# Turning the second half's attention probabilities: one set of products over 40 rows for both layers, placed behind the whole dense sum

## The chip, the cores and the metric

One NeuronCore of a Trainium2 chip runs the whole program. The metric is the device time of one execution in microseconds (us). A core has a matrix engine (TensorE, "PE" in the profile, with its weight loads listed apart as "PEld"), a vector engine (DVE), a scalar engine (ACT), a general engine (POOL), and a queue engine (SP) that issues most transfers. Each engine works through its own instructions in order; they meet at semaphores. SBUF is the on-chip memory of 128 rows (partitions); PSUM is the small memory into which PE writes its products and from which DVE and ACT copy them out.

## The reference

Two layers of memory-augmented attention, each followed by a dense block. The sequence of 2048 tokens is cut into 64 segments of 32; in front of each segment stand 8 memory tokens, which the attention itself rewrites from segment to segment, so the segments of a layer are a chain.

```python
def _A_ref(x, mem0, Wq, Wk, Wv, Wo, seg_len):      # H=32 heads, Dh=128, M=8, seg=32
    L = M + seg_len                                # 40
    mask = (idx[:, None] < M) | (idx[:, None] >= idx[None, :])
    for s in range(n_seg):
        h = concatenate([mem, xs])                 # 40 tokens
        q, k, v = h @ Wq, h @ Wk, h @ Wv           # per head
        p = softmax(where(mask, q k^T * scale, -1e9))
        o = (p v) @ Wo
        mem = o[:, :M]
        outs.append(o[:, M:])

def _B_ref(x, w1, w2):
    return relu(x @ w1) @ w2                       # 512 -> 1376 -> 512

x = x + _A_ref(_layernorm(x), ...)
x = x + _B_ref(_layernorm(x), ...)
x = x + _A_ref(_layernorm(x), ...)
x = x + _B_ref(_layernorm(x), ...)
```

## The kernel before

The two attention layers run interleaved: in step k, layer a=0 handles segment k and layer a=1 handles segment k-4. Steps 1 to 3 and 64 to 67 have one layer only, steps 4 to 63 have both; step 0 is written out apart. One step is some 23 us.

In a step the 32 heads are worked in two halves of 16. For each half, queries and keys of both layers come from one product (`qk`, line 591, 80 columns: 2 x 40 tokens), `scores` makes 40x40 scores per head and layer (line 625), and `exponentials` and `softmax` turn them into probabilities. A score tile has, per layer, two heads side by side on the partitions (rows 0 to 39 and 64 to 103, called g) and eight slots (s) in the free dimension: 128 x 8 x 40 = 128x320. The maximum, the subtraction and the row sum are on DVE (lines 643, 647, 659), the exponential on ACT (649), and the final multiplication by the reciprocal of the sum (664) on POOL, except for layer 1 of the second half, which is on DVE.

The product of probabilities and values needs the probabilities with the keys on the partitions, so they are turned. The first half's are turned by a transfer (`turn_p`, line 682). The second half's are turned on PE by `transpose_p(1, ...)`: for each of the 8 slots and each layer, a 128x64 slice of the tile `P1_sb` is loaded as weights and multiplied by an identity of 80 columns (line 675). The products of the two layers go to the two column halves of the array, so layer 0's keys land on PSUM rows 0 to 39 and layer 1's on rows 64 to 103. Two copies bring the result to `PT_sb` (line 679): ACT takes the first five slots (128x400), DVE the last three (128x240); in one-layer steps it is four and four.

Then `weighted_v` (line 701) runs 64 products, alternating between the layers (rows 0 to 39 and 64 to 103), 40 columns each. The first 16 heads read `PT0`, which the transfer filled; the last 16 read `PT_sb`, one head of each g per slot. `outputs` (719) copies the results to `OTm` (memory tokens) and `OTx` (the other tokens), `output_mem` (633, tile `wo`) multiplies `OTm` by Wo, and `new_memory` makes the next step's memory from it.

PE's work in the shadow of the softmax is the output product of the step before (`block`, 373), the dense block of an earlier segment (`dense_h`, 522; `dense_y`, 543). `dense_y` sums 11 chunks of the hidden dimension, two products of 256 columns for each chunk, in the two column halves of the array. In two-layer steps nine chunks stand ahead of the transposition and the last two behind it. `add_output(k-1)` on DVE adds the output product to the residual; it stands in DVE's order ahead of the PT copies.

The orders of PE, DVE, SP and POOL are those of the program text (`manual_schedule`, with `high_priority` blocks); ACT's is made by the scheduler. PSUM tiles come from pools: `ps_c` with three banks serves `tp`, `qp`, `vm` and some of the `pv` tiles.

`XN` is a 128x512 tile for the normalized rows. `normalize_step` fills it on DVE at the end of a step (in one-layer steps, and in step 4, early in the step itself); `transpose_step`, early in the step, turns it by a transfer into `xnT`, from which everything else reads.

The core of step k behind the second half's scores:

```python
        f_mid = 9 if ahead or k == 2 else 5
        if k < LAST:
            dense_y(k - 2, 0, f_mid)
        if not single:
            add_output(k - 1)
        ...
        with tc.high_priority(offset=PRIO):
            transpose_p(1, 4 if single else 5)
        if ahead and k < LAST:
            dense_y(k - 2, f_mid, NFC)
        tokens_in(k + 1)
        ...
            pvs = weighted_v(act)
            outputs(k, pvs)
```

Of the kernel before, what the change touches and what calls it, by code (L numbers as in the profile page):

```python
# [7 lines left out]
BF = mybir.dt.bfloat16  # L8
F32 = mybir.dt.float32
ALU = mybir.AluOpType  # L10
# [12 lines left out]
def kernel(  # L23
# [14 lines left out]
    nc = tc.nc  # L38
    _, S, Dm = A_x.shape
    _, H, Dh = A_Wq.shape[0], A_Wq.shape[1], A_Wq.shape[2]  # L40
# [4 lines left out]
    L = M + SEG  # L45
    NSEG = S // SEG
    assert NSEG % 4 == 0 and DELTA == 4
    LAST = NSEG + DELTA - 1
    NXT = NSEG // 4
    NC4 = Dm // 128  # L50
    NFC = (Dff + 127) // 128
# [5 lines left out]
    const = ctx.enter_context(tc.tile_pool(name="const", bufs=1))  # L57
    wk = ctx.enter_context(tc.tile_pool(name="wk", bufs=2))
    dram = ctx.enter_context(tc.tile_pool(name="vdram", bufs=2, space=DRAM))
    ps_c = ctx.enter_context(tc.tile_pool(name="ps_c", bufs=3, space=PSUM))  # L60
# [11 lines left out]
    def has1(k):  # L72
        return DELTA <= k <= LAST
# [22 lines left out]
    def span(d):  # L96
        offs = ([0] if has0(d) else []) + [o for o, _ in slots_of.get(d, [])]
        return base(d) + min(offs), base(d) + max(offs) + 32
# [65 lines left out]
    ident = const.tile([128, 128], BF)  # L164
# [3 lines left out]
    ident_q = ident[:].rearrange("p (g q) -> p g q", g=2)[:, :, 0:L]  # L168
# [22 lines left out]
    XN = const.tile([128, Dm], BF)  # L191
# [3 lines left out]
    Vs = const.tile([128, H * Dh], BF)  # L195
    P_sb = const.tile([128, 8, 128], BF)
    nc.gpsimd.memset(P_sb[:], 0.0)
    P1_sb = const.tile([128, 16 * L + 24], BF)
    nc.gpsimd.memset(P1_sb[:], 0.0)
    PT_sb = const.tile([128, 8, 2, L], BF)  # L200
    PT0 = const.tile([128, 8, 128], BF)
    OTx = const.tile([128, H, 64], BF)
# [6 lines left out]
    for a in range(2):  # L209
        t = ps_s.tile([128, 512], F32, name=f"sp{a}")  # L210
# [24 lines left out]
    def moments_x(n):  # L235
        return stat_tail(stats_x(n), "x")
# [295 lines left out]
    def dense_y(d, f0, f1, bank=1):  # L532
        if not 0 <= d <= LAST:
            return
        lo, hi = span(d)
        n = hi - lo
        for fc in range(NFC)[f0:f1]:
            fs = 128 if fc < NFC - 1 else F_LAST
            for j in range(2):


                w = 8 * L if fc == 0 else 256
                nc.tensor.matmul(sp_banks[bank][64 * j:64 * j + n, 0:w], lhsT=hT_tiles[d][0:fs, fc, 0:n],  # L543
                                 rhs=w2_flat[0:fs, fc * Dm + 256 * j:fc * Dm + 256 * j + w],
                                 start=(fc == 0), stop=(fc == NFC - 1), skip_group_check=True,
                                 tile_position=(0, 64 * j))
# [68 lines left out]
    def masks(*act):  # L615
        for a in act:
            nc.vector.tensor_copy(out=sp_tiles[a], in_=maskb2)  # L617
# [20 lines left out]
    def exponentials(act):  # L638
        mxs, ess = {}, {}
        for a in act:  # L640
            sp = sp_tiles[a]
            mxs[a] = wk.tile([128, 8], F32, tag="mx", bufs=2, name="mx")
            nc.vector.tensor_reduce(out=mxs[a][:], in_=sp, axis=AX.X, op=ALU.max)  # L643
        for a in act:
            sp = sp_tiles[a]
            es = ess[a] = wk.tile([128, 8, L], F32, tag="es", bufs=2, name="es")
            nc.vector.tensor_tensor(out=es[:], in0=sp, in1=mxs[a][:].unsqueeze(2).to_broadcast([128, 8, L]),  # L647
                                    op=ALU.subtract)
            last_exp[0] = nc.scalar.activation(out=es[:], in_=es[:], func=ACTF.Exp, scale=SCALE)  # L649
        return ess  # L650

    def softmax(hf, act, by_pe=False, ess=None):
        if ess is None:
            ess = exponentials(act)
        if by_pe and hf:
            transpose_p(0)
        for a, es in ess.items():
            sm = wk.tile([128, 8], F32, tag="sm", bufs=2)
            nc.vector.tensor_reduce(out=sm[:], in_=es[:], axis=AX.X, op=ALU.add)  # L659
            nc.vector.reciprocal(out=sm[:], in_=sm[:])  # L660
            eng = nc.vector if by_pe or (hf, a) == (1, act[-1]) else nc.gpsimd
            P = P1_sb[:, 0:16 * L].rearrange("p (s a q) -> p s a q", s=8, a=2)[:, :, a, :] if hf else \
                P_sb[:, :, 64 * a:64 * a + L]
            eng.tensor_tensor(out=P, in0=es[:],  # L664
                              in1=sm[:].unsqueeze(2).to_broadcast([128, 8, L]), op=ALU.mult)

    def transpose_p(hf, cut=4):

        for s0, ns, copy in ((0, cut, nc.scalar.copy), (cut, 8 - cut, nc.vector.tensor_copy)):
            tp = ps_c.tile([128, ns, 2, L], F32, tag="c", name="tp")  # L670
            for sl in range(ns):
                for a in range(2):
                    c = L * (2 * (s0 + sl) + a)
                    P = P1_sb[:, c:c + 64] if hf else P_sb[:, s0 + sl, 64 * a:64 * a + 64]
                    nc.tensor.matmul(tp[64 * a:64 * a + 64, sl], lhsT=P, rhs=ident_q,  # L675
                                     start=True, stop=True, tile_position=(0, 64 * a))
            PT = PT_sb[:, s0:s0 + ns] if hf else \
                PT0[:, s0:s0 + ns].rearrange("p s (g q) -> p s g q", g=2)[:, :, :, 0:L]
            copy(out=PT, in_=tp[:])

    def turn_p():
        nc.sync.dma_start_transpose(out=PT0[:], in_=P_sb[:].rearrange("p s k -> p (s k)"))
# [3 lines left out]
    def weighted_v(act):  # L686
        pvs = {}
        for t, (h0, nh) in enumerate(PVS):
# [6 lines left out]
            for hi in range(nh):  # L695
                hf, hh = divmod(h0 + hi, 16)
                sl, g2 = divmod(hh, 2)
                for a in act:
                    R = 64 * a
                    PT = PT_sb[R:R + L, sl, g2, :] if hf else PT0[R:R + L, sl, 64 * g2:64 * g2 + L]  # L700
                    nc.tensor.matmul(pvs[t, a][:, hi, :], lhsT=Vs[R:R + L, (h0 + hi) * Dh:(h0 + hi + 1) * Dh],  # L701
                                     rhs=PT, start=(hi == 0 or (t, a) != (1, 1)), stop=True,
                                     skip_group_check=(t, a) == (1, 1))
# [181 lines left out]
    def first_step():  # L885


        slots = iter([w1_flat[:, 512 * i:512 * i + 512] for i in range(NC4 * Dff // 512)] +
                     [w2_flat[:, 512 * i:512 * i + 512] for i in range(8)])
        masks(0)  # L890
        with tc.high_priority(offset=PRIO):
            qks = qk(0, [0])
            scores(qks, [0])
            softmax(0, [0], True)
            values_first(0)
            memory_values(0, (next(slots), None), (0,))
            values_second(0, next(slots))
            values0(1, 0, stage=next(slots))
            values0(1, 2, stage=next(slots))
            m = moments_x(2)  # L900
            normalize(nc.vector, xbs[2], xbs[2], m, 0, 128)
            inputs_T(2)
            values0(3, 0, stage=next(slots))
            values0(3, 2, stage=next(slots))
            load_x(1)
            qks = qk(1, [0], between=lambda: values0(5, 0, stage=next(slots)))
            scores(qks, [0])
            softmax(1, [0], True)
            values0(5, 2, stage=next(slots))
            values_first(1)  # L910
            memory_values(0, (None, next(slots)), (1,))
            transpose_p(1)
            tokens_in(1)
            nc.gpsimd.tensor_copy(out=HTm[:, :, 2 * M:32], in_=spare_T(1))
            values_second(1, next(slots))
            pvs = weighted_v([0])
            outputs(0, pvs)
            wo = ps_wo.tile([128, Dm], F32, tag="wo", name="wo")
            for groups, heads in zip((((1, 4),), ((1, 6),), ((3, 4),), ((3, 6), (5, 4)), ()), WO_PARTS):
                for p, n in groups:  # L920
                    values0(p, n, stage=next(slots))
                output_mem(0, wo, *heads)
            new_memory(0, [0], wo)
            output_ride(0)
            prepare(1)
# [7 lines left out]
    def step(k):  # L933
        act = layers(k)
        single = len(act) == 1
# [4 lines left out]
        ahead = has1(k + 1) or not cont  # L940
# [65 lines left out]
        else:  # L1006
# [1 line left out]
                evict_behind.append(last_exp[0].ins)  # L1008
            block(k, part, H)
            evict_behind.clear()  # L1010
        f_mid = 9 if ahead or k == 2 else 5
        if k < LAST:
            dense_y(k - 2, 0, f_mid)
        if not single:
# [5 lines left out]
        elif not single and k % 4 == 1 and has_x:  # L1020
            mom["x"] = stat_tail(mom["stats"], "x")
        with tc.high_priority(offset=PRIO):
            transpose_p(1, 4 if single else 5)
        if ahead and k < LAST:
            dense_y(k - 2, f_mid, NFC)
        tokens_in(k + 1)
        if k < LAST and spare_T(k + 1) is not None:
            nc.gpsimd.tensor_copy(out=HTm[:, :, 2 * M:32], in_=spare_T(k + 1))
# [11 lines left out]
        if cont:  # L1040
            with tc.high_priority(offset=PRIO):
                pool, tag = (ps_c, "c") if single else (ps_wo, "wo")
# [24 lines left out]
    with tc.manual_schedule(engines={mybir.EngineType.PE, mybir.EngineType.DVE, mybir.EngineType.SP,  # L1067
                                   mybir.EngineType.Pool}):
        load_rest()
        tp = transpose_pe(mem0)  # L1070
# [21 lines left out]
        R = residual(d)  # L1092
        t = xnT_tiles[d + 2] = wk.tile([128, NC4, 128], BF, tag="xnT", bufs=1, name="xnT")
# [8 lines left out]
        for fc in order:  # L1102
            fs = 128 if fc < NFC - 1 else F_LAST
            for q in range(4):
                u, j = divmod(q, 2)
                nc.tensor.matmul(sp_banks[0][32 * q:32 * q + 32, 0:256], lhsT=hT_tiles[d][0:fs, fc, SEG * u:SEG * u + SEG],  # L1106
                                 rhs=w2_flat[0:fs, fc * Dm + 256 * j:fc * Dm + 256 * j + 256],
                                 start=(fc == order[0]), stop=(fc == order[-1]), tile_position=(0, 32 * q))
        ob = wk.tile([128, 256], BF, tag="xb", bufs=1, name="ob")
        nc.vector.tensor_tensor(out=ob[:], in0=R[:, 0:256], in1=sp_banks[0][:, 0:256], op=ALU.add)  # L1110
        for u in range(2):
            r = S - SEG * (u + 1)
            for j, queue in ((0, nc.sync), (1, nc.scalar)):
                q = 64 * u + 32 * j
# [36 lines left out]
```

## Time and profile before

| | |
|---|---|
| time, median of 3 runs | 1580.35 us (1579.03 to 1581.6) |
| span of the profiled execution | 1580.0 us |
| PE busy | 1548.6 us (98%), 42866 products |
| DVE busy | 1277.3 us (81%), 3300 instructions |
| ACT busy | 734.7 us (47%) |
| POOL busy | 349.8 us (22%) |
| turning products (line 675) | 1136, 32.8 us busy |
| copies to PT_sb (679) | ACT 33.0 us, DVE 28.4 us, 68 each |
| weighted values (701) | 4096 products |
| granted PE clock | 1.000 |

The span runs from the first to the last instruction; the profile gives no other time for its execution, and the runs' median lies 0.35 us above it. A timeline row gives the start in us from the span's start, the length, the engine, the line of the kernel, the operation, what is written and read, the shape, and how many instructions are merged; a bracket at the end is idle time of the engine before it and what ended it. A weight load's form is rows*columns. A group row gives the count, the busy time, and after the comma the mean duration of one in ns.

### The profile page before, as it was taken

How to read it: one execution, taken by the hardware profiler on the slowest of the kernel's cores; microseconds unless marked ns; L12 is line 12 of the kernel's file. 1: busy time of each engine (PE TensorE's matmuls, PEld its weight loads, DVE VectorE, ACT ScalarE, POOL GpSimd, SP SyncE). 2: the span in 40 equal slices, each digit the busy share in tenths (PEclk: the TensorE clock that was granted, in tenths of full speed). 3: DMA queues.
4: the chain of work that ended last, by engine and by line, in shares of the span. 5: the costliest groups of instructions: out<-in, count | busy, mean ns of one | idle time of the engine just before them, and what ended most of it. 6: DMA issues, size and time to landing. Idle time of an engine off the chain costs nothing. (4 is left out here: it accounts for less than half of the span.)

```text
span 1580.0 us, 95139 instructions
## 1 busy us (share of the span) xinstructions
PE 1548.6 (98%) x42866; PEld 1286.3 (81%) x42866; DVE 1277.3 (81%) x3300; ACT 734.7 (47%) x1762; POOL 349.8 (22%) x670
## 2 busy tenths in 40 slices
PE   5899999999999999999999999999999999999998
PEld 3677888888888888888888888988888898888876
DVE  3578888888888888888888888888888888887866
ACT  3435445454544545454454545445454544545433
POOL 2012122222222222222122222212222221222110
PEclk9999999999999999999999999999999999999999
DMA  9734432434353244434433343443443344333331
GB/s 369 246 77 76 87 84 78 81 92 79 78 92 84 78 82 94 80 76 91 84 80 80 99 80 76 88 84 79 77 99 77 72 87 80 82 74 95 75 69 41
DMA packets 222021, 146.26 MB, mean 93 GB/s; under 512 B 123464, under 2 KB 215984, under 8 KB 221616
## 3 DMA queue, kind: packets, MB, share of 16 engines
q1 hardware_dynamic: 218448, 135.96, 38.8%
q8 instruction: 336, 5.51, 1.5%
q0 software_dynamic: 3072, 4.20, 1.1%
q14 instruction: 69, 0.57, 0.1%
q10 hardware_dynamic: 96, 0.03, 0.0%
HBM read 65.41 MB, written 45.35 MB: 70 GB/s over the span
## 5 line engine op out<-in xcount | busy, mean ns | idle before, releaser
L597 ACT CAST QT<-qp 128x480 bf16<-128x480 f32 (+3 forms) x408 | 201.5, 494 | 433.4 <-PE qp L591 433.1
L591 PE MATMUL qp<-HT,Wq_sb 128*128 128x80 bf16 (+1 forms) x8704 | 371.3, 200 | 3.2 <-POOL HT L786 1.2
L591 PEld LDWEIGHTS <-Wq_sb 128*128 128x128 bf16 x8704 | 325.9, 100 | 35.2 <-issue 27.5
L591 PE MATMUL qp<-HT,Wk_sb 128*128 128x80 bf16 (+1 forms) x8704 | 347.3, 199 | 1.7 <-issue 1.3
L591 PEld LDWEIGHTS <-Wk_sb 128*128 128x128 bf16 x8704 | 319.5, 100 | 2.6 <-issue 1.6
L664 POOL TENSOR_TENSOR P_sb<-es,sm 128x320 bf16<-128x320 f32 x185 | 130.8, 721 | 714.8 <-ACT QT L597 299.4
L599 DVE CAST KT<-qp 128x480 bf16<-128x480 f32 (+3 forms) x408 | 220.3, 565 | 36.3 <-PE qp L591 32.9
L643 DVE TENSOR_REDUCE mx<-sp 128x8 f32<-128x320 f32 x256 | 115.1, 487 | 133.1 <-PE sp L625 130.9
L373 PE MATMUL wox<-Wo_sb,OTx 128*64 128x256 bf16 x2880 | 173.6, 273 | 0.0
L373 PEld LDWEIGHTS <-OTx 128*64 128x64 bf16 x2880 | 150.2, 110 | 2.9
L649 ACT ACTIVATE es<-es 128x320 f32<-128x320 f32 x256 | 109.5, 468 | 61.9 <-DVE es L647 61.0
L797 PE MATMUL vm<-Wv_sb,HTm 128*32 128x512 bf16 x2176 | 129.4, 379 | 1.8 <-DVE KT L599 1.0
L354 PE MATMUL v<-Wv_sb,xnT 128*32 128x512 bf16 x2048 | 128.8, 378 | 0.0
L633 PE MATMUL wo<-Wo_sb,OTm 128*32 128x512 bf16 x2144 | 128.6, 380 | 0.0
L659 DVE TENSOR_REDUCE sm<-es 128x8 f32<-128x320 f32 x256 | 117.4, 459 | 13.5 <-ACT es L649 5.0
L617 DVE CAST sp<-maskb 128x320 f32<-128x320 bf16 x256 | 118.3, 483 | 0.0
L647 DVE TENSOR_TENSOR es<-sp,mx 128x320 f32<-128x320 f32 x256 | 113.6, 482 | 1.5
L543 PE MATMUL sp<-w_sb,hT 128*64 128x256 bf16 (+4 forms) x1452 | 103.9, 276 | 0.4 <-issue 0.4
L522 PE MATMUL hp<-xnT,w_sb 128*128 128x64 bf16 (+1 forms) x2948 | 98.5, 192 | 0.9 <-issue 0.5
L801 ACT CAST VmS<-vm 128x512 bf16<-128x512 f32 x134 | 78.5, 586 | 44.4 <-PE vm L797 42.5
L222 POOL TENSOR_TENSOR mv<-mv,mhalf_t 128x1 f32<-128x1 f32 x82 | 45.8, 558 | 224.6 <-DVE mv L221 218.9
L797 PEld LDWEIGHTS <-HTm 128*32 128x32 bf16 x2176 | 54.7, 97 | 48.8 <-issue 3.1
(125 smaller groups left out, 2088.5 us busy)
## 6 DMA issues: line engine op xcount, KB each, us to landing
Vs<-vd SPq DMA_DIRECT2D x96, 256.0 KB
vd<-vst SPq DMA_DIRECT2D x181, 128.0 KB
vmd<-VmS SPq DMA_DIRECT2D x134, 128.0 KB
Vs<-vmd SPq DMA_DIRECT2D x254, 32.0 KB
Vs<-vmd SPq DMA_DIRECT2D x60, 128.0 KB
Wq_sb<-in_A_Wq_dram SPq DMA_DIRECT2D x2, 2048.0 KB
Wk_sb<-in_A_Wk_dram SPq DMA_DIRECT2D x2, 2048.0 KB
Wv_sb<-in_A_Wv_dram SPq DMA_DIRECT2D x2, 2048.0 KB
```

Of the source, the lines that this page charges most:

```text
L354: nc.tensor.matmul(vp[32 * j:32 * j + 32, :], lhsT=tokens[:, c4, :], rhs=Wv_sb[:, c4, n * 512:(n + 1) * 512], start=(c4 == 0), stop=(c4 == ...
L373: nc.tensor.matmul(out[64 * j:64 * j + nr, 0:256], lhsT=lhsT, rhs=rhs[:, 256 * j:256 * j + 256], start=start, stop=stop, tile_position=(0, ...
L591: nc.tensor.matmul(qp[:, hi, 0:ncol], lhsT=W_sb[:, c4, h * Dh:(h + 1) * Dh], rhs=HT[:, c4, a_lo:a_hi, :], start=(c4 == 0), stop=(c4 == NC4 ...
L597: nc.scalar.copy(out=dst[:, 0:nh, a_lo * L:a_hi * L], in_=qp[:, 0:nh, 0:ncol])
L599: nc.vector.tensor_copy(out=dst[:, 0:nh, a_lo * L:a_hi * L], in_=qp[:, 0:nh, 0:ncol])
L617: nc.vector.tensor_copy(out=sp_tiles[a], in_=maskb2)
L633: nc.tensor.matmul(wo[32 * j:32 * j + 32, :], lhsT=OTm[:, h, n, 2 * M * c:2 * M * c + 4 * M], rhs=Wo_sb[:, h, :], start=(h < 4), stop=(h > ...
L643: nc.vector.tensor_reduce(out=mxs[a][:], in_=sp, axis=AX.X, op=ALU.max)
L647: nc.vector.tensor_tensor(out=es[:], in0=sp, in1=mxs[a][:].unsqueeze(2).to_broadcast([128, 8, L]), op=ALU.subtract)
L659: nc.vector.tensor_reduce(out=sm[:], in_=es[:], axis=AX.X, op=ALU.add)
L664: eng.tensor_tensor(out=P, in0=es[:], in1=sm[:].unsqueeze(2).to_broadcast([128, 8, L]), op=ALU.mult)
L797: nc.tensor.matmul(vp[32 * j:32 * j + 32, :], lhsT=HTm[:, c4, :], rhs=Wv_sb[:, c4, n * 512:(n + 1) * 512], start=(c4 == 0), stop=(c4 == NC ...
```

## The change

The probabilities of the second half are kept in two tiles of four slots each: slots 0 to 3 lie in `XN`, slots 4 to 7 in a smaller `P1_sb`. A slot is 104 columns wide: layer 0's 40 keys at column 0, layer 1's at column 64. The multiplication that writes them is therefore issued as two instructions of 128x160 for each layer in place of one of 128x320.

`turn_second` replaces `transpose_p(1, ...)`. For each slot and each g it loads the 40 rows of that g and all 104 columns as weights and multiplies by a 40x40 identity: 16 products of 40 columns, alternating between rows 0 to 39 and rows 64 to 103, where before there were 16 of 80 columns. The results of g=0 go to one PSUM tile and those of g=1 to another. Four copies of 104x160 bring them to `PT_sb`, two on ACT (g=0) and two on DVE (g=1).

All eleven chunks of `dense_y` stand ahead of it in the two-layer steps. `transpose_p` remains for the few first-half transpositions that are made on PE.

```diff
-    P1_sb = const.tile([128, 16 * L + 24], BF)
+    PW1 = 64 + L
+    P1_sb = const.tile([128, 4 * PW1], BF)
     nc.gpsimd.memset(P1_sb[:], 0.0)
+    P1 = [t[:, 0:4 * PW1].rearrange("p (s k) -> p s k", s=4) for t in (XN, P1_sb)]
...
             eng = nc.vector if by_pe or (hf, a) == (1, act[-1]) else nc.gpsimd
-            P = P1_sb[:, 0:16 * L].rearrange("p (s a q) -> p s a q", s=8, a=2)[:, :, a, :] if hf else \
-                P_sb[:, :, 64 * a:64 * a + L]
-            eng.tensor_tensor(out=P, in0=es[:],
-                              in1=sm[:].unsqueeze(2).to_broadcast([128, 8, L]), op=ALU.mult)
+            if not hf:
+                eng.tensor_tensor(out=P_sb[:, :, 64 * a:64 * a + L], in0=es[:],
+                                  in1=sm[:].unsqueeze(2).to_broadcast([128, 8, L]), op=ALU.mult)
+                continue
+            for u in range(2):
+                eng.tensor_tensor(out=P1[u][:, :, 64 * a:64 * a + L], in0=es[:, 4 * u:4 * u + 4],
+                                  in1=sm[:, 4 * u:4 * u + 4].unsqueeze(2).to_broadcast([128, 4, L]), op=ALU.mult)
+
+    def turn_second():
+
+        tps = [ps_c.tile([128, 8, L], F32, tag="c", name="tp") for _ in range(2)]
+        for u in range(2):
+            for sl in range(4):
+                for g in range(2):
+                    R = 64 * g
+                    nc.tensor.matmul(tps[g][0:PW1, 4 * u + sl, :], lhsT=P1[u][R:R + L, sl, :],
+                                     rhs=ident[R:R + L, R:R + L], start=True, stop=True)
+        for u in range(2):
+            for g, copy in ((0, nc.scalar.copy), (1, nc.vector.tensor_copy)):
+                copy(out=PT_sb[0:PW1, 4 * u:4 * u + 4, g, :], in_=tps[g][0:PW1, 4 * u:4 * u + 4, :])
...
-        f_mid = 9 if ahead or k == 2 else 5
+        f_mid = NFC if ahead else 9 if k == 2 else 5
...
         with tc.high_priority(offset=PRIO):
-            transpose_p(1, 4 if single else 5)
-        if ahead and k < LAST:
-            dense_y(k - 2, f_mid, NFC)
+            turn_second()
         tokens_in(k + 1)
```

More of the change, by code (lines that the diff above doesn't have):

```diff
@@ L655, in softmax @@
         if by_pe and hf:
-            transpose_p(0)
+            transpose_p()
         for a, es in ess.items():
@@ L661, in softmax @@
             eng = nc.vector if by_pe or (hf, a) == (1, act[-1]) else nc.gpsimd
-            P = P1_sb[:, 0:16 * L].rearrange("p (s a q) -> p s a q", s=8, a=2)[:, :, a, :] if hf else \
-                P_sb[:, :, 64 * a:64 * a + L]
-            eng.tensor_tensor(out=P, in0=es[:],
-                              in1=sm[:].unsqueeze(2).to_broadcast([128, 8, L]), op=ALU.mult)
[L667 to L671, printed above, removed]
+            if not hf:
+                eng.tensor_tensor(out=P_sb[:, :, 64 * a:64 * a + L], in0=es[:],
+                                  in1=sm[:].unsqueeze(2).to_broadcast([128, 8, L]), op=ALU.mult)
+                continue
@@ L672, in transpose_p @@
+    def transpose_p():
+        for s0, copy in ((0, nc.scalar.copy), (4, nc.vector.tensor_copy)):
+            tp = ps_c.tile([128, 4, 2, L], F32, tag="c", name="tp")
+            for sl in range(4):
                 for a in range(2):
-                    c = L * (2 * (s0 + sl) + a)
-                    P = P1_sb[:, c:c + 64] if hf else P_sb[:, s0 + sl, 64 * a:64 * a + 64]
-                    nc.tensor.matmul(tp[64 * a:64 * a + 64, sl], lhsT=P, rhs=ident_q,
+                    nc.tensor.matmul(tp[64 * a:64 * a + 64, sl], lhsT=P_sb[:, s0 + sl, 64 * a:64 * a + 64], rhs=ident_q,
@@ L676, in transpose_p @@
                                      start=True, stop=True, tile_position=(0, 64 * a))
-            PT = PT_sb[:, s0:s0 + ns] if hf else \
-                PT0[:, s0:s0 + ns].rearrange("p s (g q) -> p s g q", g=2)[:, :, :, 0:L]
-            copy(out=PT, in_=tp[:])
+            copy(out=PT0[:, s0:s0 + 4].rearrange("p s (g q) -> p s g q", g=2)[:, :, :, 0:L], in_=tp[:])
     def turn_p():
@@ L911, in first_step @@
             memory_values(0, (None, next(slots)), (1,))
-            transpose_p(1)
+            turn_second()
             tokens_in(1)
@@ L1022, in step @@
         with tc.high_priority(offset=PRIO):
-            transpose_p(1, 4 if single else 5)
-        if ahead and k < LAST:
-            dense_y(k - 2, f_mid, NFC)
+            turn_second()
         tokens_in(k + 1)
```

## The prediction

> **What bounds the kernel now.** I read the page first, for which engine is full, and then the timelines of PE, DVE and ACT around one transposition, for what ends last there.
>
> ```profile
> span 1580.0 us, 95139 instructions
> PE 1548.6 (98%) x42866; PEld 1286.3 (81%) x42866; DVE 1277.3 (81%) x3300; ACT 734.7 (47%) x1762; POOL 349.8 (22%) x670
> PE   5899999999999999999999999999999999999998
> ```
>
> PE is full from the second slice to the end. A step is a fixed sequence on PE, so whatever PE saves in a step, or loses by waiting, is in the total once for each of the 67 steps behind step 0. A two-layer step, on PE:
>
> ```profile
> 813.80 1.45 PE L522 MATMUL hp<-xnT,w_sb 128*128 128x64 bf16 x44
> 818.55 1.18 PE L543 MATMUL sp<-w_sb,hT 128*64 128x320 bf16 x18
> 819.56 0.46 PE L675 MATMUL tp<-ident,P_sb 128*64 128x80 bf16 x16
> 819.85 0.39 PE L543 MATMUL sp<-w_sb,hT 128*64 128x256 bf16 x4
> 820.17 0.49 PE L701 MATMUL pv<-PT,Vs 40*128 40x40 bf16 x25
> ...
> 820.79 0.36 PE L701 MATMUL pv<-PT_sb,Vs 40*128 40x40 bf16 x16
> 821.08 1.91 PE L633 MATMUL wo<-Wo_sb,OTm 128*32 128x512 bf16 x32
> 823.68 0.27 PE L857 MATMUL mt<-sel,wm 128*32 128x16 bf16 x16
> ```
>
> I count from the first transposition, 819.56, as 0. The dense tail starts at 0.29, the weighted values (pv) at 0.61, wo at 1.52. The same step on DVE and ACT:
>
> ```profile
> 815.60 0.89 DVE L643 TENSOR_REDUCE mx<-sp 128x8 f32<-128x320 f32 x2 [1.18 <-PE sp L625]
> 818.77 0.63 DVE L664 TENSOR_TENSOR P_sb<-es,sm 128x320 bf16<-128x320 f32 x1
> 819.43 0.85 DVE L379 TENSOR_TENSOR R<-R,wox 64x256 f32<-64x256 f32 x2
> 820.31 0.41 DVE L679 CAST PT_sb<-tp 128x240 bf16<-128x240 f32 x1
> 820.67 0.73 DVE L719 CAST OTm<-pv 128x96 bf16<-128x96 f32 x3
> ```
>
> ```profile
> 819.95 0.49 ACT L679 CAST PT_sb<-tp 128x400 bf16<-128x400 f32 x1 [2.17 <-PE tp L675]
> 820.71 0.24 ACT L719 CAST OTm<-pv 128x96 bf16<-128x96 f32 x1 [0.27 <-PE pv L701]
> 820.84 0.48 ACT L719 CAST OTx<-pv 128x384 bf16<-128x384 f32 x1
> 823.04 0.59 ACT L849 CAST wm<-wo 128x512 bf16<-128x512 f32 x1 [0.79 <-PE wo L633]
> ```
>
> The copies to PT_sb are late but covered: ACT's ends at 0.88, DVE's at 1.16. PE first needs ACT's at head 16 (0.61 + 16 x 0.026 = 1.03) and DVE's, slots 5 to 7, only at head 26 (1.29). DVE has no pause from the multiplication to OTm. Releasing PE after a copy takes 0.05: wm ends at 823.63, mt starts at 823.68. In two other steps wo starts at 1.54 and 1.55; in the one at 796.46 add_output does nothing, and DVE is free early and waits for the products:
>
> ```profile
> 796.46 0.48 PE L675 MATMUL tp<-ident,P_sb 128*64 128x80 bf16 x16
> 798.00 1.26 PE L633 MATMUL wo<-Wo_sb,OTm 128*32 128x512 bf16 x20
> ```
>
> ```profile
> 773.92 0.46 PE L675 MATMUL tp<-ident,P_sb 128*64 128x80 bf16 x16
> 775.47 1.26 PE L633 MATMUL wo<-Wo_sb,OTm 128*32 128x512 bf16 x20
> ```
>
> ```profile
> 796.98 0.41 DVE L679 CAST PT_sb<-tp 128x240 bf16<-128x240 f32 x1 [0.39 <-PE tp L675]
> 797.59 0.73 DVE L719 CAST OTm<-pv 128x96 bf16<-128x96 f32 x3 [0.20 <-PE pv L701]
> ```
>
> There the copy starts 0.52 after the first product. The last of the sixteen starts at 0.48 - 0.20 = 0.28, so a copy begins 0.24 behind the start of the last product it waits for: its duration (0.20) and 0.04.
>
> **The change part by part.** *Moving the dense tail.* Its four products take the same time ahead as behind. They are two pairs, 0.11 apart (18 in 819.56 - 818.55 = 1.01, nine pairs). Behind the second pair PE goes from 128x64 tiles to 40x128 ones, and pv started 0.32 after the tail's first product, 0.21 after its second pair: 0.10 more than a pair's pitch. I take that as the price of changing the tile's shape. It is paid once before and once after, now ahead of the turn, which has pv's shape of rows. So the turn starts at 0.11 + 0.21 = 0.32. But the tail no longer runs between the transposition and pv: it was 0.32 of cover for the copies.
>
> *The sixteen products.* Before, eight pairs at (0.46 - 0.20) / 7 = 37 ns. For 40 rows by 104 columns of weights against 40 moving columns no row exists. The nearest:
>
> ```profile
> L633 PEld LDWEIGHTS <-OTm 128*32 128x32 bf16 x2144 | 53.7, 96 | 45.1 <-ACT OTm L719 2.5 <-issue 1.2 <-DVE OTm L719 0.4
> L675 PEld LDWEIGHTS <-P_sb 128*64 128x64 bf16 x1136 | 27.5, 111 | 6.7 <-DVE P_sb L664 2.0 <-issue 1.1 <-POOL HT L786 0.2
> L701 PEld LDWEIGHTS <-Vs 40*128 40x128 bf16 x4096 | 59.3, 93 | 14.3 <-issue 14.0 <-DMA xT<-xb 0.2
> L701 PE MATMUL pv<-PT_sb,Vs 40*128 40x40 bf16 x1536 | 37.3, 177 | 0.0
> ```
>
> The pv pairs, alike in rows and moving columns, come every (0.36 - 0.18) / 7 = 26 ns; that is the lower end. Their loads of 128 columns are short (93), shorter than those of 64 (111); from 32 to 64 columns a load grows by 15 ns, 0.47 ns a column. If 104 columns lie on that slope, a load holds its path for 49 ns. Loads of the two halves can run beside each other: two loads of 64 columns would take 60 ns in turn, and the pairs came every 37. So 47 to 49 ns a pair if the row halves do too, 94 to 98 if they take turns. Only the full width shows the short load, so I take the slope, side by side: 0.047. Eight pairs: 0.38, against 0.29 before. Halving the moving columns then saves nothing: the load sets the pitch.
>
> The Trainium skill ("TensorE: Matmul & The Clock Gate", Weight-path perf modes) grants the fast weight load only where the number of weights is 128, which speaks against 104 columns; the two load rows above agree with it. The same page (LDWEIGHTS) gives a load as its columns divided by 1.2 GHz, which would be an estimated 87 ns for 104 columns; by that the pair's pitch would be 0.087 and the total about 1613. The trace disagrees: by it 64 columns are 53 ns, and pairs with such loads came every 37.
>
> *The copies.* In the built program the first of each engine's two copies carries the wait for PE and the second none, so the first waits for all sixteen products. The last pair starts at 0.32 + 7 x 0.047 = 0.65, its products take 0.18, and the copies start at 0.65 + 0.18 + 0.04 = 0.87. For 160 columns:
>
> ```profile
> L599 DVE CAST KT<-qp 128x160 bf16<-128x160 f32 x16 | 5.0, 315 | 0.1
> L599 DVE CAST KT<-qp 128x320 bf16<-128x320 f32 x120 | 58.1, 485 | 0.1
> L597 ACT CAST QT<-qp 128x160 bf16<-128x160 f32 x16 | 4.7, 293 | 17.1 <-PE qp L591 17.1
> L643 DVE TENSOR_REDUCE mx<-sp 128x8 f32<-128x320 f32 x256 | 115.1, 487 | 133.1 <-PE sp L625 130.9 <-PE qp L591 2.2
> ```
>
> Two neighbours overlap by 0.08 on DVE (2 x 0.487 against 0.89) and by 0.11 on ACT (OTx starts 0.11 before OTm ends). DVE's copies end at 1.19 and 1.42, ACT's at 1.16 and 1.35. pv starts at 0.32 + 0.38 = 0.70. Head 17 (the first of g=1) would come at 0.70 + 17 x 0.026 = 1.14 and waits until 1.19 + 0.05 = 1.24. Head 25 would come at 1.45 and waits until 1.47. The last pair starts at 1.47 + 6 x 0.026 = 1.63. Before, wo started 0.11 behind the last pair (820.79 + 7 x 0.026 = 820.97 to 821.08), so now at 1.74, which is the copies' start plus 0.87. It was 1.52 to 1.55. DVE's OTm copies begin behind 1.42, and the first (0.26) ends at 1.68, with release 1.73: just covered; it is late next if anything on DVE grows.
>
> *The split multiplications.* On DVE one of 0.63 becomes two. Of it 0.15 is fixed, if it is as in the KT copies above (0.315 for 160 columns, 0.170 more for 320), so two cost 0.78 less the overlap 0.08: 0.07 more; bounds 0 and 0.15. That ends ahead of the turn (819.47 against 819.88), and add_output behind it ends at 0.79, ahead of 0.87: nothing, as long as the turn ends so late. With a short turn those 0.07 are on the path. POOL's half for layer 0:
>
> ```profile
> 818.33 0.71 POOL L664 TENSOR_TENSOR P_sb<-es,sm 128x320 bf16<-128x320 f32 x1 [3.74 <-DVE sm L660]
> ```
>
> Even if each half cost the whole, it would end at 819.75, ahead of 819.88; behind it POOL only fetches the next step's tokens. Nothing.
>
> *The norm tile.* Its transfer had to land before `hp` at 813.80, 4.5 us before the first write of probabilities, and the next normalization follows wo. The added waits hold up nobody.
>
> **Sum.** 1.74 against 1.52, 1.54 and 1.55 is +0.21 a step, rounded (0.22 to 0.19). The one-layer steps have the same copies and the same turn; I count them alike: 67 x 0.21 = 14 us. On the profiled 1580.0, or the median 1580.35 that stands 0.35 above it: 1594.4.
>
> **The rivals.** *Short loads.* If 104 columns load as fast as 128, pairs come every 0.026: copies from 0.72, wo at 1.59 where DVE is free; where add_output and the split hold DVE until 0.82, wo at 1.69. Mean +0.11: 1587.6. For it: pv's rows; against it: the 64-column load is not short.
>
> *Loads in turn.* 0.094 a pair: copies from 1.20, wo at 2.07, +0.54: 1616. Against it: column halves load side by side; for it: no row shows long loads in two row halves.
>
> *A longer vector chain.* Splits and copies at their upper bounds (0.15 and no overlap) put OTm behind pv and cost some 0.08 more a step: about 1600.
>
> *Hidden copies, faster.* With pairs at 0.026, pv starts at 0.53 in place of 0.61, and if no copy held it wo would start at 0.53 + 31 x 0.026 + 0.11 = 1.45, -0.08 a step: 1575. It decides from the point where the first copies begin by 0.55 and the second are done by 1.1; for it, PE needs nothing of PT_sb for 16 heads; against it, DVE is not free before 0.72 in the first step shown.
>
> *Nothing to measure*: short loads, and waits that just give the 0.08 back: within 0.2% (3 us), about what a measurement of this kernel can tell.
>
> **How the numbers follow.** Slope and side by side 0.50; short loads 0.17; longer vector chain 0.10; in turn 0.10; hidden 0.08; nothing 0.05. Faster 0.08, same 0.05, slower 0.87. The forecast is the likeliest, 1594.4. The range takes in short loads with a little less waiting below (1584) and stops, above, short of loads in turn, at a pitch of some 70 ns (1608).
>
> **What would show it.** The turn's sixteen products start 0.32 behind the tail's first, and eight pairs last about 0.38; loads of 40x104 read about 125 to 130 ns. pv shows a pause at head 17, ended by DVE's PT_sb copy, and wo starts 1.74 behind the tail. The step grows by about 0.21. It is wrong if the pairs come every 26 ns, if copies start before the eighth pair, or if pv runs without a pause.

## The result, and the profile after

The changed kernel takes 1601.95 us (median of 4 runs, 1601.47 to 1603.34), the kernel before beside it 1580.97 us (1579.03 to 1582.09). The ratio is 1.0135, with a 95% interval of 1.012 to 1.015: 21 us slower, 0.31 us for each of the 67 steps. The prediction was 1594.4 us, and 1584 to 1608.

From the page after:

```profile
span 1600.5 us, 95522 instructions
PE 1569.2 (98%) x42866; PEld 1305.7 (82%) x42866; DVE 1296.4 (81%) x3436; ACT 727.9 (45%) x1830; POOL 358.6 (22%) x730
PEclk9999999999999999999999999999999999999999
```

PE issues the same number of products, at the same clock. It only looks busier: a pause shorter than the 0.18 us that such a product lasts leaves no idle time in the profile, because the product before it is still running. Where the time goes is seen in the timeline of PE, in a step like the first one of the prediction:

```profile
733.10 1.39 PE L545 MATMUL sp<-w_sb,hT 128*64 128x320 bf16 x22
734.43 0.37 PE L679 MATMUL tp<-ident,XN 40*104 40x40 bf16 x8
734.64 0.35 PE L679 MATMUL tp<-ident,P_sb 40*104 40x40 bf16 x8
734.84 0.48 PE L715 MATMUL pv<-PT,Vs 40*128 40x40 bf16 x25
...
735.21 0.18 PE L715 MATMUL sp<-PT,Vs 40*128 40x40 bf16 x1
735.37 0.18 PE L715 MATMUL pv<-PT_sb,Vs 40*128 40x40 bf16 x1
735.43 0.18 PE L715 MATMUL pv<-PT_sb,Vs 40*128 40x40 bf16 x1
...
735.61 0.43 PE L715 MATMUL pv<-PT_sb,Vs 40*128 40x40 bf16 x16
735.67 0.37 PE L715 MATMUL pv<-PT_sb,Vs 40*128 40x40 bf16 x15
735.97 0.61 PE L635 MATMUL wo<-Wo_sb,OTm 128*32 128x512 bf16 x6
```

(The row at 735.67 is from a narrower window: it counts again 15 of the 16 products of the row above it. The row `sp<-PT` is a product of layer 1 that uses a PSUM bank of the scores for its result.)

I count from the first turn product, 734.43, as 0. pv starts at 0.41. It pauses from 735.21 to 735.37, ahead of head 16, and again until 735.43, ahead of head 17. The last sixteen products, heads 24 to 31, take 0.43 in place of 0.36: a third pause stands between the two products of head 24, from 735.61 to 735.67. wo starts at 1.54. The two copying engines in the same step:

```profile
733.32 0.32 DVE L669 TENSOR_TENSOR XN<-es,sm 128x160 bf16<-128x160 f32 x1
733.56 0.57 DVE L669 TENSOR_TENSOR P_sb<-es,sm 128x160 bf16<-128x160 f32 x1
734.17 0.85 DVE L381 TENSOR_TENSOR R<-R,wox 64x256 f32<-64x256 f32 x2
735.06 0.56 DVE L683 CAST PT_sb<-tp 104x160 bf16<-104x160 f32 x2
```

```profile
735.02 0.48 ACT L683 CAST PT_sb<-tp 104x160 bf16<-104x160 f32 x2 [2.69 <-PE tp L679]
```

ACT's first copy (0.295 mean) ends at 735.32 and head 16 runs at 735.37; DVE's first (0.32) ends at 735.38 and head 17 runs at 735.43; DVE's second ends at 735.62 and head 24's second product runs at 735.67. Each pause ends 0.05 behind a copy.

Head 24 itself reads only what ACT copied (g=0). By the order in which the tiles take the three banks of `ps_c` (both `tp`, then the `pv` tiles), the result of its second product goes into the bank that DVE's second copy has just emptied; that is a reading of the program, and it fits the time. The groups of the turn:

```profile
L679 PE MATMUL tp<-ident,P_sb 40*104 40x40 bf16 x544 | 23.7, 199 | 0.0
L679 PEld LDWEIGHTS <-P_sb 40*104 40x104 bf16 x544 | 18.6, 125 | 0.0
```

A load of 40x104 lasts 125 ns. Eight products span 0.35 with one of 0.199 in it: three gaps between pairs, (0.35 - 0.20) / 3 = 0.05 us each.

### The profile page after: what moved, and what is told of

The parts are those of the page before. It is cut to its first block, busy times and chain, and to the rows that moved or that the text cites. A ratio compares the mean times of both kernels' runs of the same rounds, so it can differ in the third digit from the quotient of the medians.

```text
span 1600.5 us, 95522 instructions
## 1 busy us (share of the span) xinstructions
PE 1569.2 (98%) x42866; PEld 1305.7 (82%) x42866; DVE 1296.4 (81%) x3436; ACT 727.9 (45%) x1830; POOL 358.6 (22%) x730
## 4 chain that ended last, share of the span: by engine, by line
PE 96%; DMA 2%; DVE 1%; SPq 1%; issue 1%; ACT 0%; POOL 0%; POOLq 0%
PE qp L593 38%; PE wox L375 10%; PE wo L635 8%; PE vm L811 7%; PE v L356 7%; PE hp L524 5%; PE sp L545 5%; PE pv L715 4%; PE sp L627 4%; PE vp L312 3%; PE tp L679 2%; DMA Wv_sb<-in_A_Wv_dram 2%; PE sp L715 1%; PE wox L398 1%; SPq L134 0%
## 5 line engine op out<-in xcount | busy, mean ns | idle before, releaser
L665 POOL TENSOR_TENSOR P_sb<-es,sm 128x320 bf16<-128x320 f32 x125 | 87.8, 722 | 505.0 <-ACT QT L599 338.1
L683 ACT CAST PT_sb<-tp 104x160 bf16<-104x160 f32 x136 | 33.0, 295 | 150.4 <-PE tp L679 150.4
```

## The experiments

The theory has three parts: the turn's loads of 104 columns set the pace of its products, the tail behind the transposition was cover for the copies, and PE now waits for these copies. The parts were taken out one by one. The kernel before was run again beside each set of runs, and a ratio is to those runs.

**Slots of 128 columns.**

```diff
-    PW1 = 64 + L
+    PW1 = 128
```

> The changed kernel with slots of 128 columns in place of 104, so that the turn's weight loads have the full width. Theory (the length of the 104-column loads sets the pitch of the turn's pairs, 48 ns in the trace of the changed kernel): pairs every 26 ns, the turn lasts about 0.24 us instead of 0.41, and wo starts some 0.18 us earlier in the half of the steps in which add_output does not hold DVE; in the other half DVE's copies cannot start before add_output ends, and nothing is gained. Mean 0.09 us x 67 steps: about 1596 us, between the changed kernel's 1602 and the 1581 of before. Rival (the loads do not matter, the lost cover and the number of copies do): 1602, pitch unchanged.

Measured: 1596.96 us, ratio to before 1.0095 (1.0078 to 1.0111). The loads as a group row, then two steps of PE and of DVE:

```profile
L679 PEld LDWEIGHTS <-P_sb 40*128 40x128 bf16 x544 | 11.6, 93 | 0.1
```

```profile
707.94 0.27 PE L679 MATMUL tp<-ident,XN 40*128 40x40 bf16 x8
709.28 0.62 PE L635 MATMUL wo<-Wo_sb,OTm 128*32 128x512 bf16 x8
...
731.17 0.27 PE L679 MATMUL tp<-ident,XN 40*128 40x40 bf16 x8
731.39 0.51 PE L715 MATMUL pv<-PT,Vs 40*128 40x40 bf16 x25
732.70 0.40 PE L635 MATMUL wo<-Wo_sb,OTm 128*32 128x512 bf16 x4
```

```profile
708.38 0.56 DVE L683 CAST PT_sb<-tp 128x160 bf16<-128x160 f32 x2 [0.38 <-PE tp L679]
...
730.90 0.85 DVE L381 TENSOR_TENSOR R<-R,wox 64x256 f32<-64x256 f32 x2
731.79 0.56 DVE L683 CAST PT_sb<-tp 128x160 bf16<-128x160 f32 x2
```

Loads with 23% more columns take 93 ns instead of 125, and the turn lasts 0.22 (731.17 to 731.39) instead of 0.41. Where DVE waits for PE (708.38), wo starts 1.34 behind the turn's start instead of 1.54; where add_output holds DVE until 731.75, it starts at 1.53 and nothing is gained. The rival, that the loads do not matter, falls.

**Only the dense sum moved, in the kernel before.**

```diff
-        f_mid = 9 if ahead or k == 2 else 5
+        f_mid = NFC if ahead else 9 if k == 2 else 5
```

> The kernel before with nothing changed but the whole dense sum ahead of the old transposition. Theory (the dense tail was cover for the copies): the transposition starts 0.22 us later, ACT's copy of five slots ends at 1.10 and head 16 waits for it some 0.13 us; wo starts 0.13 us later in each of the 60 two-layer steps: about 1588 us. Rival (the 16 first heads of the weighted values are cover enough, the order costs nothing): 1581 us, and no pause at head 16.

Measured: 1589.55 us, ratio 1.0044 (1.0029 to 1.0059), 7 us. PE and ACT in one step:

```profile
707.09 0.45 PE L675 MATMUL tp<-ident,P_sb 128*64 128x80 bf16 x16
707.48 0.49 PE L701 MATMUL pv<-PT,Vs 40*128 40x40 bf16 x25
708.02 0.18 PE L701 MATMUL pv<-PT_sb,Vs 40*128 40x40 bf16 x1
708.52 0.40 PE L633 MATMUL wo<-Wo_sb,OTm 128*32 128x512 bf16 x4
```

```profile
707.48 0.49 ACT L679 CAST PT_sb<-tp 128x400 bf16<-128x400 f32 x1 [0.83 <-PE tp L675]
```

ACT's copy ends at 707.97, but the sixteen heads that begin at 707.48 are issued by 707.90; head 16 runs at 708.02, 0.05 behind the copy. wo starts 1.43 behind the transposition, which itself stands 0.22 later: 1.65 where it was 1.52 to 1.55. The lost cover, by itself and in the kernel before, costs 7 us, a third of what the whole change costs. The rival, that the order costs nothing, falls.

**The tail put back behind the turn.**

```diff
-        f_mid = NFC if ahead else 9 if k == 2 else 5
+        f_mid = 9 if ahead or k == 2 else 5
...
             turn_second()
+        if ahead and k < LAST:
+            dense_y(k - 2, f_mid, NFC)
```

> The changed kernel with the last two chunks of the dense sum put back behind the turn. Theory (a change of the tile's shape on PE costs 0.10 us, and there are now three of them around the turn in place of one): the copies are covered, no pause at heads 16, 17 and 24, but pv starts at 0.10 + 0.41 + 0.10 + 0.11 + 0.21 = 0.93 us behind the ninth chunk, against 0.61 before: +0.32 us a step, so about 1601 us, the same as the changed kernel within 2 us. Rival (the shape changes are free, only waiting counts): +0.12 us a step, about 1588 us.

Measured: 1603.52 us, ratio 1.0137 (1.012 to 1.0154). In its timeline of PE the pauses are gone, and nothing is won:

```profile
734.92 1.17 PE L545 MATMUL sp<-w_sb,hT 128*64 128x320 bf16 x18
736.02 0.37 PE L679 MATMUL tp<-ident,XN 40*104 40x40 bf16 x8
...
736.51 0.41 PE L545 MATMUL sp<-w_sb,hT 128*64 128x256 bf16 x4
736.86 0.49 PE L715 MATMUL pv<-PT,Vs 40*128 40x40 bf16 x25
737.77 0.40 PE L635 MATMUL wo<-Wo_sb,OTm 128*32 128x512 bf16 x4
```

The turn starts 0.20 behind the last product ahead of it (734.92 + 1.17 - 0.27 = 735.82), where a pair's pitch is 0.11. From its start to the tail's 0.49 passes, where the turn lasts 0.41 when pv follows it. pv starts at 736.86, 0.93 behind the place where the next dense pair would have stood (735.82 + 0.11), which is just what the expectation worked out with 0.10 for each change of the tile's shape. wo stands 1.75 behind the turn's start. So three such changes cost what the waits cost, and the rival, that they are free, falls.

**Only the split of the multiplications, in the kernel before.**

```diff
-            eng.tensor_tensor(out=P, in0=es[:],
-                              in1=sm[:].unsqueeze(2).to_broadcast([128, 8, L]), op=ALU.mult)
+            for s0 in (0, 4) if hf else (0,):
+                ns = 4 if hf else 8
+                eng.tensor_tensor(out=P[:, s0:s0 + ns], in0=es[:, s0:s0 + ns],
+                                  in1=sm[:, s0:s0 + ns].unsqueeze(2).to_broadcast([128, ns, L]), op=ALU.mult)
```

> The kernel before with nothing changed but the second half's multiplication by the reciprocal issued as two instructions of 128x160 per layer. Theory (these end ahead of the products that read them, and what they add on DVE is covered): 1581 us, within 2 us. Rival (they lengthen DVE's chain, which is full up to OTm): +0.07 to +0.15 us a step, 1586 to 1591 us.

Measured: 1593.36 us, ratio 1.0069 (1.0054 to 1.0084), 11 us: my expectation was wrong, and it is above the rival's 1586 to 1591 too. DVE and PE in one step:

```profile
821.83 0.94 DVE L666 TENSOR_TENSOR P_sb<-es,sm 128x160 bf16<-128x160 f32 x2
823.68 0.41 DVE L681 CAST PT_sb<-tp 128x240 bf16<-128x240 f32 x1
```

```profile
822.62 0.53 PE L677 MATMUL tp<-ident,P_sb 128*64 128x80 bf16 x16
824.14 0.35 PE L703 MATMUL pv<-PT_sb,Vs 40*128 40x40 bf16 x15
```

Two halves take 0.94 where the whole took 0.63. They end at 822.77, when the transposition has already begun, so its products wait for the second half and take 0.53 in place of 0.46. DVE's copy then ends at 824.09. It holds slots 5 to 7, which are first read by head 26, but PE stops earlier: the last 15 of the 64 products, from head 24's second one on, start at 824.14, 0.05 behind the copy. This is the third pause of the changed kernel again, in the order of the kernel before.

Two further kernels split the multiplication on one engine each, with the condition `eng is nc.vector` or `eng is nc.gpsimd` in the loop. Each was run once.

> The kernel before with only DVE's multiplication (layer 1, second half) split in two, POOL's left whole. In the kernel with both split DVE's two instructions took 0.61 and 0.41 us against 0.63 for the whole one. Theory (DVE's multiplication runs slower while POOL works on SBUF at the same time, whatever its length, so halves of it do not take half): with POOL's instruction whole and over earlier, the first half takes some 0.5 to 0.6 and the second some 0.33 to 0.41. Rival (an instruction of 160 columns simply takes 0.41 or more): both 0.41 or more whatever POOL does.

> The kernel before with only POOL's multiplication (layer 0, second half) split in two, DVE's left whole. Theory (DVE is slowed by the time it shares with POOL): POOL's two halves take 0.44 each in place of 0.71 for the whole, DVE's multiplication runs beside POOL for longer and takes 0.65 to 0.8 us in place of 0.63. Rival (no sharing): 0.63 unchanged.

Measured: 1584.82 us with DVE split and 1591.37 us with POOL split, beside 1583.69 for one run of the kernel before. POOL and DVE with DVE split:

```profile
819.14 0.71 POOL L667 TENSOR_TENSOR P_sb<-es,sm 128x320 bf16<-128x320 f32 x1 [3.68 <-DVE sm L660]
819.81 0.38 POOL L789 COPY HT<-xT 128x128 bf16<-128x128 bf16 x1
```

```profile
819.58 0.79 DVE L667 TENSOR_TENSOR P_sb<-es,sm 128x160 bf16<-128x160 f32 x2
```

and with POOL split:

```profile
845.41 0.86 POOL L667 TENSOR_TENSOR P_sb<-es,sm 128x160 bf16<-128x160 f32 x2 [3.92 <-DVE sm L660]
```

```profile
845.85 0.77 DVE L667 TENSOR_TENSOR P_sb<-es,sm 128x320 bf16<-128x320 f32 x1
```

```profile
846.77 0.48 PE L678 MATMUL tp<-ident,P_sb 128*64 128x80 bf16 x16
```

```profile
L678 PEld LDWEIGHTS <-P_sb 128*64 128x64 bf16 x1136 | 27.6, 111 | 14.6 <-issue 11.8 <-DVE P_sb L667 2.0 <-POOL HTm L1031 0.2
```

DVE's instruction ends a fixed time behind POOL's, not a fixed time behind its own start: the whole one at 846.62, 0.35 behind POOL's 846.27; the second half at 820.37, 0.18 behind POOL's copy, 820.19. So it is POOL's later end that makes DVE's part long. The kernel with DVE split shows it in one run: the second half takes 0.41 where POOL's copy runs beside it, and 0.31 in the steps that have no such copy (one begins at 796.96). Both rivals fall. Both times are single runs. With DVE split alone the difference is 1 us, which is within the noise. With POOL split it is 8 us. There the transposition comes late: it starts 0.15 behind the end of DVE's multiplication in most steps (846.77 behind 846.62 here), and 0.23 behind the last dense product ahead of it, where that was 0.11 in the kernel before. The idle time ahead of its weight loads is 14.6 us in all, where it was 6.7. The 8 us more of it are the whole difference. The profile names no releaser for most of this time; that DVE's longer multiplication causes it is read from the fixed 0.15 alone.

**One tile, no split, the turn unchanged.**

```diff
-    XN = const.tile([128, Dm], BF)
-    nc.vector.memset(XN[:], 0.0)
+    both = const.tile([128, 8 * PW1], BF)
+    nc.gpsimd.memset(both[:], 0.0)
+    XN = both[:, 0:Dm]
...
+    P1 = both[:].rearrange("p (s k) -> p s k", s=8)
...
+            eng.tensor_tensor(out=P1[:, :, 64 * a:64 * a + L], in0=es[:],
+                              in1=sm[:].unsqueeze(2).to_broadcast([128, 8, L]), op=ALU.mult)
```

> The changed kernel with XN and the probabilities in one tile of 832 columns, so that the multiplication is again one instruction of 128x320 per layer; the turn is unchanged. Theory (DVE's copies start 0.63 us behind the turn's start for two reasons at once, the end of the sixteenth product and the end of add_output): taking the split away frees DVE some 0.19 us earlier, but PE then holds the copies at the same place: the changed kernel's time within 3 us, ratio to before 1.012 to 1.0135. Rival (the split costs here what it cost alone in the kernel before, 10 us): ratio about 1.007.

Measured: 1603.79 us, ratio 1.0141 (1.0113 to 1.017). DVE and PE in a step with add_output:

```profile
733.85 0.69 DVE L667 TENSOR_TENSOR both<-es,sm 128x320 bf16<-128x320 f32 x1
735.58 0.56 DVE L681 CAST PT_sb<-tp 104x160 bf16<-104x160 f32 x2 [0.16 <-PE tp L677]
```

```profile
734.95 0.56 PE L677 MATMUL tp<-ident,both 40*104 40x40 bf16 x16
```

The split, worth 11 us alone in the kernel before, is worth nothing in the changed one. There the turn stands behind the whole dense sum, so the probabilities are ready in time; and DVE, free earlier without the split, now waits 0.16 for the turn's last products and starts its copies 0.63 behind the turn's start, as before. The rival, that the split costs here what it cost alone, falls.

**No split and wide slots together**: the same with `PW1 = 128`.

> The kernel with one tile and one multiplication per layer, and slots of 128 columns. Theory (the turn's length and the split hold DVE's copies in parallel, so only taking both away pays in all steps): wo about 0.18 us earlier than in the changed kernel in all steps, 12 us less, ratio to before about 1.006. Rival (the two savings simply add up where each has its effect, the wide slots' 0.004 and nothing from the split): 1.009.

Measured: 1591.03 us, ratio 1.005 (1.0035 to 1.0066): 13 us less than the same tile with 104 columns. PE in a step with add_output:

```profile
684.57 0.37 PE L677 MATMUL tp<-ident,both 40*128 40x40 bf16 x16
685.98 0.83 PE L634 MATMUL wo<-Wo_sb,OTm 128*32 128x512 bf16 x12
```

wo starts 1.41 behind the turn's start here, where the wide slots alone gave up to 1.53, and 1.34 to 1.35 in the steps in which DVE is free early. So all steps gain, and the rival of simple addition falls. It is the best of the new forms, and still slower than before. What is left, 9 us, is about what moving the dense sum cost alone (7 us); that it is the same loss is not shown.

**Each copy behind its own eight products.** The copies of slots 0 to 3 are written ahead of the products of slots 4 to 7, in the changed kernel and in the wide one without split:

```diff
         for u in range(2):
             for sl in range(4):
                 ...
-        for u in range(2):
             for g, copy in ((0, nc.scalar.copy), (1, nc.vector.tensor_copy)):
```

> The changed kernel with the copies of slots 0 to 3 written ahead of the products of slots 4 to 7, so that each copy waits for its own eight products. Theory (the copies start too late because the first waits for all sixteen; on DVE they also wait for add_output in half of the steps): ACT's first copy starts 0.19 us earlier everywhere. Where add_output ends late DVE's copies start as before and wo gains nothing; in the other half wo comes 0.16 to 0.24 us earlier. Mean 0.10 us x 67: 6.7 us less than the changed kernel, a ratio to before of about 1.009. Rival (PE is bound by the turn's loads alone): 1.0135, unchanged.

> One tile, one multiplication per layer, slots of 128 columns, and each copy waiting for its own eight products. Theory: PE still waits at head 16 (0.05 us), 17 (0.1 us) and 25, because the turn, its copies and the release together are longer than the 0.40 us of the sixteen heads that stand in front; wo comes 0.20 to 0.26 us earlier than in the changed kernel and some 0.1 us later than before: ratio to before about 1.004. If the waits vanish wholly: 0.08 us a step less than before, ratio 0.997.

Measured: 1642.12 us, ratio 1.0375 (1.0353 to 1.0396), and 1630.86 us, 1.0302 (1.028 to 1.0323). Both expectations missed by more than 40 us. PE and ACT in the first:

```profile
778.84 0.37 PE L679 MATMUL tp<-ident,XN 40*104 40x40 bf16 x8
779.58 0.46 PE L679 MATMUL tp<-ident,P_sb 40*104 40x40 bf16 x8 [0.38 <-ACT PT_sb L682]
```

```profile
779.24 0.29 ACT L682 CAST PT_sb<-tp 104x160 bf16<-104x160 f32 x1 [2.49 <-PE tp L679]
```

The ninth product starts 0.05 behind the end of ACT's copy (779.53) and 0.74 behind the first product, though it writes other columns than the copy reads. The Trainium skill ("PSUM — Partial Sum Buffer", PSUM bank collisions raise a hardware error) states that two engines must not use the same bank and the same quarter of its rows at once, and that a dependency is put between any two such instructions. Here the copies read the banks that the next products write, and that fits the wait which the trace shows; each `tp` tile fills a bank of its own, so no run tells a wait for the bank from a wait for the tile. ACT's copy did start earlier, 0.40 behind the turn's start in place of 0.59. Halves in separate banks would need four, and `ps_c` has three; that variant wasn't tried.

## Why the prediction was right, and where it was short

- *The tail and the shape.* The turn was to start 0.32 behind the tail's first product. The last product of the dense sum starts at 733.10 + 1.39 - 0.27 = 734.22 and the turn 0.21 later: as predicted. That a change of the tile's shape costs some 0.10 is borne out by the kernel with the tail put back, where three of them were forecast to put pv at 0.93 and did.
- *The loads.* Predicted: loads of 125 to 130 ns and a pair every 47 to 49 ns, side by side. Measured: 125 ns, and about 50 ns. The wide slots show the cause: with loads of 93 ns the turn lasts 0.22.
- *The waits.* Predicted at heads 17 and 25 behind DVE's copies; measured at heads 16 and 17 and at head 24's second product. The pause at head 16 followed from my own figures: ACT's first copy ends at 1.16, with release at 1.21, and head 16 would come at 0.70 + 16 x 0.026 = 1.12. I overlooked it; it adds nothing, since head 17 waits longer. The third pause I put one head too late, because I asked only who reads PT_sb and not whose bank the result goes into. The same slip is in my reading of the kernel before: PE needs DVE's copy there not at head 26 (1.29) but at head 24 (1.23), so the cover was 0.02 and not 0.08. Predicted copies from 0.87 behind the tail's start, wo at 1.74; measured 0.32 + 0.63 = 0.95 on DVE (735.06) and 0.32 + 1.54 = 1.86 for wo.
- *The term that was too small* is this wait, 0.12 us of 0.33. The turn's products last 0.199, not pv's 0.177; its first pairs come slower, so that it lasts 0.41 and not 0.38; DVE's copy starts 0.07 behind the last product's end and not 0.04; and the pauses with the last pairs and the way to wo take 0.91 from DVE's copy on, where I had 0.87, mostly because the third pause has one more pair behind it. All four errors have the same sign. Together they are 0.12 x 67 = 8 us, which is what 1594.4 lacks.
- *The split.* Sized at 0.07 on DVE, covered. It is 0.57 + 0.32 less the overlap: from 733.32 to 734.13, 0.81 against 0.63, so 0.18. The cover holds nevertheless, as the kernel without the split shows: add_output ends just before the turn's copies could start anyway. It held by a margin of 0.04 at most: DVE is free at 735.02, and the copies start at 735.06.
- *The rivals.* Short loads, loads in turn, and hidden copies are all settled by the two load rows, the pitch of 0.05 and the pauses. POOL's split costs nothing that shows: the kernel with one tile, in which it is gone, has the same time. No run takes away the sharing of the norm tile. The traces speak against a cost: from wo to the next step's turn 21.88 us pass, where it was 21.57 (medians of the two-layer steps), and the 0.31 between them is the dense tail that now stands there.

## What to carry to other kernels

Halving the moving columns of a small product saves nothing if the weight load then sets the pitch, and a wider load can be the shorter one: 128 columns took 93 ns here, 104 took 125. A step moved ahead of a transposition takes away cover from the copies behind it: count the time until the first reader, the time until the slowest copy, and also who needs the bank that the copy empties. Two delays that hold the same point in parallel show little or nothing when one of them is taken out; take both out together before calling either free.

## What was not expected of the hardware

A DVE multiplication with two SBUF inputs that POOL's work holds up ends 0.35 us (320 columns) or 0.18 us (160) behind the end of the POOL instruction beside it, in the steps shown. Before the change the whole one took 0.63 with POOL beside it, and 0.49 in the one-layer step at 1507.10, where POOL has nothing to do at that time. The Trainium skill ("SBUF — State Buffer", SBUF: two separate sides) has the two engines share a pair of ports under a lock for the whole instruction, for a DVE operation with two SBUF inputs against a POOL operation that reads SBUF; the trace agrees: 320 columns at the 0.170 for 160 that the KT copies of the prediction give would be an estimated 0.34, so DVE does its pass only when POOL has ended. Cutting such an instruction in two on POOL ends POOL's part later and therefore lengthens DVE's, here from 0.63 to 0.77.
